# One plan table of a fused linear-attention and feed-forward kernel: own, state and past products put in one place

## The chip, the cores and the metric

The kernel runs on one core of a Trainium2 chip. The metric is the device time of one execution in microseconds (us), as the median over runs. Half a per cent of it (2.7 us) is about what a measurement of this kernel can tell from no change.

## The reference

A recurrence over 768 steps for 4 batches and 8 heads of width 48, and a feed-forward layer with a cosine gate on its output:

```python
for t in range(S):
    cur = u[None] * kt outer vt
    y[:, :, t] = rt . (state + cur)
    state = wt[:, :, :, None] * state + kt outer vt
x = y as (3072 tokens, 384)
h = x @ w_in            # 384 -> 2048
out = (h * cos(h)) @ w_out   # 2048 -> 384
```

Both weights and everything else are float32.

## The kernel before, in words

The 768 steps are cut into 24 chunks of 128 steps (6 per batch, `order`). Two chunks of the same place in two batches make a block (`BLK = 2`), so there are 12 blocks, 0 to 11.

For a chunk, the attention part has these steps, each named by a letter in the plan: `load` (the transposed r, k and w come by DMA into a tile `tt`, five of these), `lr` and `lv` (r and k again for the diagonal, tile `rk`; v, tile `v`, four of these), `decay` (two scans along the chunk on VectorE and the scaling of r and k by them), `diag` (the terms of u: products of `rk` summed to `cd`, L229 to L232, and spread by GpSimd on the diagonal of the score tile `asb`, L236, four of these), `a` (scores k·r on TensorE, L259, then copied under a mask into `asb`, L261), `t` (transposes of k, L268) and `d` (the carried state times the chunk's decay, `dd`, L249, copied to the tiles `past`). For a block it has `o` (the own products: scores times v, L314 and L319, into the banks `py`), `p` (the past products: carried state times r, L329 and L333, added into the same `py`, and then `xT` made from `py`: the high part by ScalarE, the rest by VectorE at L144), and `s` (the state products k·v, L286, into `pst`, then the new state `sn`, L293).

The feed-forward part of a block is 8 units of 256 hidden columns. `mm1` of a unit is 18 matmuls (L382: each product is split in high and low parts, three passes) from `xT` into one of three banks `ph`. A gate follows: L357 on ScalarE, L358 on VectorE, L359 on ScalarE, L360 on VectorE; then `gs`, the high part by a cast on ScalarE and the low part by two subtractions on GpSimd (L144). There are two `gs` tiles, so the cast of unit n waits for `mm2` of unit n-2. `mm2` is 12 matmuls (L401) into `acc`; the first 8 read the high part, the last 4 the low part. `mm2` runs `LAG = 3` units behind `mm1`.

TensorE's order is written out by hand: `START` for the first part, and from then on the eight rows of `PLAN`, one per unit, over and over. A step in a row is emitted where it stands, unless `NEEDS` or the buffer rules in `att` pull it forward: `lv+6` pulls `o` and `s` of the block whose v tile it will overwrite, and a `load` pulls `o`, `s` and `p`. The other engines' orders come from the scheduler, which follows the order of emission and the readiness of data. Rows of `PLAN` set the places for the own products of blocks 3 to 11 (nine blocks); blocks 0 to 2 have theirs in `START`. Blocks 10 and 11 have no state products, since nothing comes after them.

```python
        elif n == "lv":
            att((j - BUFS["v"]) // BLK, "o")
            att((j - BUFS["v"]) // BLK, "s")
```

Of the kernel before, what the change touches and what calls it, by code (L numbers as in the profile page):

```python
# [52 lines left out]
PLAN = ["t+2 t+3 load+6 mm1 mm2",  # L53
        "a+2 mm2 mm1 decay+4",
        "mm2 a+3 mm1 diag+4",
        "mm1 o+1 mm2 diag+5 p+1 lv+6 lr+7 x+2",
        "mm1 s+1 mm2 load+7 lv+7 x+3",
        "mm1 mm2 d+4",
        "mm1 mm2 decay+5",
        "mm1 d+5 mm2 lr+6"]  # L60
# [7 lines left out]
             o="a lv", s="t d lv", p="o d")  # L68
# [637 lines left out]
```

## Time and profile before

| | |
|---|---|
| median of 3 runs | 546.23 us (544.84 to 546.92) |
| the profiled execution | 547.09 us |
| its span in the trace | 545.4 us |
| TensorE (PE) busy | 516.6 us, 95% |
| VectorE (DVE) busy | 368.1 us, 68% |
| ScalarE (ACT) busy | 270.7 us, 50% |
| GpSimd (POOL) busy | 205.0 us, 38% |
| mean granted clock of TensorE | 0.995 |

The span starts with the first instruction in the trace and ends with the last; the profiled execution's own time has 1.7 us more. Times in the rows below are microseconds from the start of the span. PE is the matmuls, PEld the weight loads that run ahead of them. Matmuls overlap in the pipeline, so of a group of matmuls the distance from its start to the start of the next group tells what it costs, rather than its own length.

### The profile page before, as it was taken

The numbers are of one execution on the slowest core, as the hardware profiler recorded it, in microseconds if no ns is written. First come the engines' busy times: TensorE is split into PE (matmuls) and PEld (weight loads), VectorE is DVE, ScalarE is ACT, GpSimd is POOL, SyncE is SP. The second block draws the span as 40 slices with busy tenths as digits, with TensorE's granted clock in tenths as the row PEclk, the third lists the DMA queues.
The fourth block names the chain that finished last, engine by engine and source line by source line (L and its number), as shares of the span: only waits on it lengthen the run. The fifth ranks groups of instructions, "written<-read, shape, count | busy, mean of one in ns | idle before, by whom it ended". The sixth has DMA issues, their size and how long they took to land. (4 is left out here: it accounts for less than half of the span.)

```text
span 545.4 us, 11929 instructions
## 1 busy us (share of the span) xinstructions
PE 516.6 (95%) x4980; PEld 492.9 (90%) x4980; DVE 368.1 (68%) x568; ACT 270.7 (50%) x456; POOL 205.0 (38%) x274
## 2 busy tenths in 40 slices
PE   3668999999899999999999999999999999999996
PEld 3666989989899999999999999999999999999996
DVE  7988999978787477478478478468468664433331
ACT  1778999645343444344444444344344345344542
POOL 4141336653344335335334334334334334323332
PEclk9999999999899999999999999999999999999999
DMA  8984771204370060061061051052032330000000
GB/s 269 277 303 167 240 220 41 77 7 132 117 180 16 30 183 12 30 171 25 30 170 26 30 150 46 30 148 48 29 106 99 131 131 1 31 1 1 30 2 31
DMA packets 16440, 51.38 MB, mean 94 GB/s; under 512 B 1984, under 2 KB 8384, under 8 KB 16384
## 3 DMA queue, kind: packets, MB, share of 16 engines
q1 hardware_dynamic: 16240, 50.49, 30.9%
q8 instruction: 40, 0.66, 0.5%
q14 instruction: 16, 0.13, 0.1%
q10 hardware_dynamic: 144, 0.10, 0.1%
HBM read 45.87 MB, written 4.72 MB: 93 GB/s over the span
## 5 line engine op out<-in xcount | busy, mean ns | idle before, releaser
L144 POOL TENSOR_TENSOR gs<-rr,gs 128x256 fp32r<-128x256 f32 x192 | 159.0, 850 | 228.3 <-ACT gs L141 220.1
L382 PE MATMUL ph<-xT,w 128*128 128x256 f32 x1728 | 225.2, 285 | 6.3 <-ACT w L141 4.8
L382 PEld LDWEIGHTS ph<-xT,w 128*128 128x128 f32 x1728 | 216.5, 192 | 9.8 <-ACT w L141 5.3
L401 PE MATMUL acc<-w,gs 128*128 128x384 f32 x1152 | 218.7, 339 | 1.0 <-DVE rr L360 1.0
L401 PEld LDWEIGHTS acc<-w,gs 128*128 128x128 f32 x1152 | 196.1, 188 | 4.6 <-issue 3.0
L359 ACT ACTIVATE rr<-rr,quarter 128x512 f32<-128x512 f32 x96 | 69.4, 723 | 110.2 <-DVE rr L358 110.0
L358 DVE SCALAR_TENSOR_TENSOR rr<-rr,ph 128x512 f32<-128x512 int32 x96 | 65.5, 682 | 76.2 <-ACT rr L357 63.3
L360 DVE TENSOR_TENSOR rr<-rr,ph 128x512 f32<-128x512 f32 x96 | 65.4, 682 | 46.8 <-ACT rr L359 46.8
L357 ACT ACTIVATE rr<-ph 128x512 int32<-128x512 f32 x96 | 57.1, 595 | 57.6 <-PE ph L382 57.4
L141 ACT CAST gs<-rr 128x512 fp32r<-128x512 f32 x96 | 59.0, 615 | 50.8 <-PE acc L401 40.3
L236 POOL TENSOR_SCALAR_AFFINE_SELECT asb<-cd 128x512 f32<-128x512 f32 x48 | 33.7, 733 | 50.6 <-ACT cd L141 25.6
L261 DVE COPY_PREDICATED asb<-mask,pa 128x512 f32<-128x512 uint8 x48 | 32.9, 735 | 5.8 <-PE pa L259 5.8
L259 PE MATMUL pa<-tt 48*128 48x128 f32 x384 | 32.6, 311 | 1.6 <-ACT ob L414 1.4
L259 PEld LDWEIGHTS pa<-tt 48*128 48x128 f32 x384 | 27.1, 210 | 6.8 <-issue 4.4
L208 DVE TENSOR_TENSOR_SCAN ee<-tt,one_e 112x516 f32<-112x516 f32 x24 | 31.4, 1308 | 1.8 <-DMA tt<-tr 1.8
L213 DVE TENSOR_TENSOR_SCAN tt<-tt,inj 112x516 f32<-112x516 f32 x24 | 31.3, 1303 | 0.1
L141 POOL COPY wholes<-ee 112x4 f32<-112x4 f32 x24 | 10.5, 438 | 54.1 <-DVE ee L208 54.1
L141 ACT COPY past<-dd 48x192 f32<-48x192 f32 x40 | 14.0, 351 | 21.9 <-DVE dd L249 21.3
L224 PEld LDWEIGHTS pc<-u_by_head,rkt 112*128 112x128 f32 x64 | 11.1, 259 | 14.8 <-DVE rkt L205 8.6
L224 PE MATMUL pc<-u_by_head,rkt 112*128 112x2 f32 x64 | 11.3, 299 | 13.6 <-DVE rkt L205 13.1
L217 DVE TENSOR_TENSOR tt<-tt 112x512 f32<-112x512 f32 x24 | 20.0, 833 | 0.1
L229 DVE TENSOR_TENSOR rk<-rk 128x384 f32<-128x384 f32 x16 | 10.9, 680 | 12.4 <-DMA rk<-tn 12.4
(65 smaller groups left out, 346.4 us busy)
## 6 DMA issues: line engine op xcount, KB each, us to landing
tt<-tr SPq DMA_DIRECT2D x22, 674.2 KB, 7.3
raw<-wts SPq DMA_DIRECT2D x16, 768.0 KB, 5.9
rk<-tn SPq DMA_DIRECT2D x16, 384.0 KB, 3.3
v<-tv SPq DMA_DIRECT2D x24, 224.0 KB, 7.0
ww<-w SPq DMA_DIRECT2D x6, 768.0 KB, 4.3
out<-ob SPq DMA_DIRECT2D x23, 192.0 KB, 2.0
tt<-tr SPq DMA_DIRECT2D x4, 224.0 KB, 4.3
tt<-tr SPq DMA_DIRECT2D x2, 226.2 KB, 3.5
```

Source lines behind the costliest of these rows:

```text
L141: (nc.scalar.copy if E[name] is nc.scalar else E[name].tensor_copy)(out=out, in_=in_)
L144: E[name].tensor_tensor(out=out, in0=full, in1=high.bitcast(F32), op=ALU.subtract)
L208: nc.vector.tensor_tensor_scan(out=ee.rearrange("p a t -> p (a t)")[:, ::-1], data0=wp[:, 1:W129 + 1][:, ::-1], data1=one_e.rearrange("p a ...
L236: nc.gpsimd.affine_select(out=asb, in_=col.unsqueeze(2).to_broadcast([C, NP, C]), pattern=[[0, 4], [1, C]], compare_op=ALU.is_equal, fill= ...
L259: nc.tensor.matmul(out=pa[h][:, p], lhsT=a["k3"][rows(h), p], rhs=a["r3"][rows(h), p], start=True, stop=True)
L261: nc.vector.copy_predicated(a["asb", h], mask, pa[h])
L357: nc.scalar.activation(nn, ph, AF.Copy, scale=INV2PI / W_SCALE, bias=0.25)
L358: nc.vector.scalar_tensor_tensor(out=rr, in0=nn, scalar=-2.0 * math.pi * W_SCALE, in1=ph, op0=ALU.mult, op1=ALU.add)
L359: nc.scalar.activation(rr, rr, AF.Sin, scale=1.0 / W_SCALE, bias=quarter)
L360: nc.vector.tensor_tensor(out=rr, in0=rr, in1=ph, op=ALU.mult)
L382: nc.tensor.matmul(out=ph[:, fi], lhsT=wgt[u * FU + fi][:, 0, a, kt * 128:(kt + 1) * 128], rhs=xT[:, b, kt], start=n == 0, stop=n == 3 * K ...
L401: nc.tensor.matmul(out=accs[i][j][:, :DM], lhsT=gs[:, a, fi, j * C:(j + 1) * C], rhs=wgt[u * FU + fi][:, 1, b], start=u == 0 and fi == 0 a ...
```

## The change

Two rows of the plan table are written differently; nothing else is.

```diff
 PLAN = ["t+2 t+3 load+6 mm1 mm2",
         "a+2 mm2 mm1 decay+4",
         "mm2 a+3 mm1 diag+4",
-        "mm1 o+1 mm2 diag+5 p+1 lv+6 lr+7 x+2",
-        "mm1 s+1 mm2 load+7 lv+7 x+3",
+        "mm1 mm2 diag+5 lv+6 lr+7",
+        "mm1 o+1 p+1 s+1 mm2 x+2 load+7 lv+7 x+3",
         "mm1 mm2 d+4",
```

In TensorE's order, in a block in the middle, between `mm1` of unit 3 (the two weight tiles w6 and w7) and `mm1` of unit 4 (w8), there stood before (`py` are the own and past products' banks, `pst` the state's):

```order
L382 MATMUL ph_2130<-xT_1738,w7_616 128x256 x9
L314 MATMUL py_2162<-asb_1614,v_2158 32x128 x2
...
L319 MATMUL py_2163<-asb_1704,v_2160 32x128 x4
L401 MATMUL acc_2196<-w0_181,gs_1989 128x384
...
L329 MATMUL py_2162<-tt_1529,past0_91 32x128 x4
L333 MATMUL py_2162<-tt_1529,past0_91 32x128 x4
...
L286 MATMUL pst_2247<-v_2158,kn_1954 64x48
...
L382 MATMUL ph_2274<-xT_1738,w8_670 128x256 x9
```

and in the same place there stands now:

```order
L382 MATMUL ph_2130<-xT_1761,w7_616 128x256 x9
L401 MATMUL acc_2158<-w0_181,gs_1989 128x384
...
L314 MATMUL py_2184<-asb_1614,v_2180 32x128 x2
...
L319 MATMUL py_2185<-asb_1670,v_2182 32x128 x4
L286 MATMUL pst_2218<-v_2180,kn_1954 64x48
...
L329 MATMUL py_2184<-tt_1529,past0_91 32x128 x4
L333 MATMUL py_2184<-tt_1529,past0_91 32x128 x4
...
L382 MATMUL ph_2274<-xT_1761,w8_670 128x256 x9
```

The own products moved behind the 12 matmuls of `mm2` of unit 0. The state and past products kept their place ahead of `mm1` of unit 4, but the state products, which `lv+6` pulls, now come before the past products, which `lr+7` pulls through its `load`. So `mm1` and `mm2` touch here, and own, state and past products follow one another.

On GpSimd, around the spreading of the diagonal (L236) in a later block, there stood before (`gs_3122` is the low part of unit 2, `gs_3158` that of unit 3):

```order
L144 TENSOR_TENSOR gs_3057<-rr_3052,gs_3057 128x256 x2
L236 AFFINE_SELECT asb_3130<-cd_3128 128x512
...
L236 AFFINE_SELECT asb_3216<-cd_3212 128x512
L144 TENSOR_TENSOR gs_3122<-rr_3117,gs_3122 128x256 x2
L141 COPY wholes_86<-ee_3561 112x4
L141 COPY wholes_86<-ee_3900 112x4
L144 TENSOR_TENSOR gs_3158<-rr_3153,gs_3158 128x256 x2
```

and now:

```order
L144 TENSOR_TENSOR gs_3057<-rr_3052,gs_3057 128x256 x2
L144 TENSOR_TENSOR gs_3122<-rr_3117,gs_3122 128x256 x2
L236 AFFINE_SELECT asb_3130<-cd_3128 128x512
...
L236 AFFINE_SELECT asb_3182<-cd_3178 128x512
L141 COPY wholes_86<-ee_3561 112x4
L141 COPY wholes_86<-ee_3900 112x4
L144 TENSOR_TENSOR gs_3158<-rr_3153,gs_3158 128x256 x2
```

The low part of unit 2 moved ahead of the four spreadings, which therefore come later.

On VectorE, behind those spreadings, in the block of the first pair of fences, the order was (`rr_2293` is the gate of unit 4, `rr_2335` that of unit 5; the second scan L208 reads the tile `tt_2270`):

```order
L232 TENSOR_REDUCE cd_2628<-rk_2451 128x8
...
L229 TENSOR_TENSOR rk_2772<-rk_2772 128x384
...
L229 TENSOR_TENSOR rk_2951<-rk_2951 128x384
...
L358 SCALAR_TENSOR_TENSOR rr_2293<-rr_2293,ph_2274 128x512
L213 SCALAR_TENSOR_TENSOR tt_1963<-tt_1963,inj_80 112x516
L208 SCALAR_TENSOR_TENSOR ee_2900<-tt_2270,one_e_77 112x516
L360 TENSOR_TENSOR rr_2293<-rr_2293,ph_2274 128x512
...
L358 SCALAR_TENSOR_TENSOR rr_2335<-rr_2335,ph_2316 128x512
L213 SCALAR_TENSOR_TENSOR tt_2270<-tt_2270,inj_80 112x516
```

and is now:

```order
L232 TENSOR_REDUCE cd_2628<-rk_2451 128x8
...
L213 SCALAR_TENSOR_TENSOR tt_1963<-tt_1963,inj_80 112x516
L229 TENSOR_TENSOR rk_2772<-rk_2772 128x384
L358 SCALAR_TENSOR_TENSOR rr_2293<-rr_2293,ph_2274 128x512
L217 TENSOR_TENSOR tt_1963<-tt_1963 112x512
L208 SCALAR_TENSOR_TENSOR ee_2900<-tt_2270,one_e_77 112x516
L360 TENSOR_TENSOR rr_2293<-rr_2293,ph_2274 128x512
...
L213 SCALAR_TENSOR_TENSOR tt_2270<-tt_2270,inj_80 112x516
L230 TENSOR_TENSOR rk_2772<-rk_2772,u_sb_84 128x384
L358 SCALAR_TENSOR_TENSOR rr_2335<-rr_2335,ph_2316 128x512
```

So L358 of unit 5 moved behind the second L213, and one of the two products L229 moved behind L358 of unit 5. `sn` and `dd`, which stood behind `xT`, now stand ahead of it. SP's queue changed with them: per block it held `out` twice, `rk` twice, `tt`, `v` twice, `tt`; it now holds `rk`, `v`, `tt`, `v`, `tt`, `rk`, `out` twice.

## Rows read from the trace of the kernel before

**Rows 1.** Windows: length, busy of PE, PEld, DVE, ACT, POOL, clock, DMA, GB/s.
```profile
230.00:275.00 45.00, 45.00 (x493) 43.06 (x495) 29.25 (x47) 19.57 (x35) 15.81 (x23) 1.00 0.25 69
```
**Rows 2.** Timeline of PE, 224 to 254: start, length, group, count.
```profile
224.66 2.25 PE L401 MATMUL acc<-w,gs 128*128 128x384 f32 x12
226.84 1.16 PE L259 MATMUL pa<-tt 48*128 48x128 f32 x16
227.94 4.47 PE L382 MATMUL ph<-xT,w 128*128 128x256 f32 x36
232.34 0.64 PE L314 MATMUL py<-asb,v 128*32 128x128 f32 x16
...
234.22 2.37 PE L401 MATMUL acc<-w,gs 128*128 128x384 f32 x12
236.52 0.64 PE L329 MATMUL py<-tt,past 112*32 112x128 f32 x16
...
237.69 1.13 PE L286 MATMUL pst<-v,kn 128*64 128x48 f32 x32
238.75 2.37 PE L382 MATMUL ph<-xT,w 128*128 128x256 f32 x18
240.96 2.25 PE L401 MATMUL acc<-w,gs 128*128 128x384 f32 x12
243.05 2.26 PE L382 MATMUL ph<-xT,w 128*128 128x256 f32 x18
245.15 2.25 PE L401 MATMUL acc<-w,gs 128*128 128x384 f32 x12
...
253.52 1.73 PE L401 MATMUL acc<-w,gs 128*128 128x384 f32 x9
```
**Rows 3.** Timeline of PEld, same block; in brackets idle before, and why.
```profile
232.69 0.46 PEld L319 LDWEIGHTS py<-asb,v 128*32 128x32 f32 x16
...
234.22 2.05 PEld L401 LDWEIGHTS acc<-w,gs 128*128 128x128 f32 x12 [0.20 <-issue]
236.52 0.38 PEld L329 LDWEIGHTS py<-tt,past 112*32 112x32 f32 x16 [0.25 <-issue]
```
**Rows 4.** Timeline of ACT, same block.
```profile
236.70 0.62 ACT L141 CAST gs<-rr 128x512 fp32r<-128x512 f32 x1 [2.13 <-PE acc L401]
...
250.84 0.60 ACT L141 CAST gs<-rr 128x512 fp32r<-128x512 f32 x1
```
**Rows 5.** Timeline of POOL, same block.
```profile
233.31 2.40 POOL L236 TENSOR_SCALAR_AFFINE_SELECT asb<-cd 128x512 f32<-128x512 f32 x4 [3.34 <-PE py L319]
237.40 1.42 POOL L144 TENSOR_TENSOR gs<-rr,gs 128x256 fp32r<-128x256 f32 x2 [1.69 <-ACT gs L141]
```
**Rows 6.** Timeline of DVE, same block.
```profile
234.57 0.55 DVE L232 TENSOR_REDUCE cd<-rk 128x8 f32<-128x384 f32 x1 [0.75 <-POOL asb L236]
...
238.25 0.98 DVE L229 TENSOR_TENSOR rk<-rk 128x384 f32<-128x384 f32 x1 [1.95 <-DMA rk<-tn]
...
243.42 0.66 DVE L218 TENSOR_TENSOR tt<-tt,ee 112x512 f32<-112x512 f32 x1
...
248.45 1.13 DVE L218 TENSOR_TENSOR tt<-tt,ee 112x512 f32<-112x512 f32 x1
249.50 0.67 DVE L358 SCALAR_TENSOR_TENSOR rr<-rr,ph 128x512 f32<-128x512 int32 x1
250.10 1.22 DVE L213 TENSOR_TENSOR_SCAN tt<-tt,inj 112x516 f32<-112x516 f32 x1
```
**Rows 7.** DMA issues at 237.6 and at 239.2: size, us to landing.
```profile
tt<-tr SPq DMA_DIRECT2D x1, 674.2 KB, 7.0
...
tt<-tr SPq DMA_DIRECT2D x1, 674.2 KB, 9.2
```
**Rows 8.** Timeline of PE, 142 to 150: a wait ahead of scores, then two mm1.
```profile
142.49 1.19 PE L259 MATMUL pa<-tt 48*128 48x128 f32 x14 [1.42 <-ACT ob L414]
143.61 5.98 PE L382 MATMUL ph<-xT,w 128*128 128x256 f32 x36
```

## The prediction

> **What bounds the kernel now.** First the windows: in a stretch of 45 us in the middle TensorE is busy for all 45, VectorE for 29, ScalarE for 20 and GpSimd for 16, at the full granted clock [rows 1]. So TensorE is the bound there, and nothing is to be won by making another engine faster. Then its timeline, where busy can hide small losses: I read the distance from the start of a group to the start of the next [rows 2]. An `mm1` behind an `mm2` takes 2.10 us (243.05 to 245.15), one behind float32 products of other shapes 2.21 (238.75 to 240.96). An `mm2` takes 2.18 between an `mm1` and other products (224.66 to 226.84), 2.30 between two kinds of other products (234.22 to 236.52). So each change of kind costs about 0.1 us on either side of it. The weight loads show the same: inside the own products they follow without a pause, and at a change they idle 0.20 to 0.25 us [rows 3]. The last view is of the other engines behind the own products, since they hold the gates that TensorE needs later [rows 4 to 6].
>
> **The change on TensorE.** No matmul is added or removed; one `mm2` and the own products change places, and state and past products do. Per block:
> - The two `mm1` of units 2 and 3 take 4.40 us before (227.94 to 232.34), because own products follow. Now `mm2` follows: 2.21 + 2.10 = 4.31 [rows 2]. Gain 0.09.
> - `mm2` of unit 0 stood between own and past products, 2.30; now it stands between `mm1` and own products, 2.18. Gain 0.12.
> - Own (1.88), past (1.17) and state products (1.06) stay as long, by the starts of [rows 2]. Each of the three ended on a change of kind or shape before, which its distance contains, and each does now.
>
> That is 0.21 us in each of the nine blocks that the table places: 9 x 0.21 = 1.9 us. In blocks 10 and 11, which have no state products, own and past products of one width now touch; what that saves is nothing at least and one pause of 0.20 each at most [rows 3], 0 to 0.4 together. I take 0.2. The changes from own to state and from state to past products are in no row. The nearest are the pauses of 0.20 and 0.25 [rows 3]; a change may cost one pause more or one less than the one that it replaces, so 7 x 0.2 = 1.4 us to either side in the seven blocks with state products. I take none, since every change of shape in the rows lies within 0.05 us of the others. Sum: 2.1 us, with bounds of 0.5 and 3.7.
>
> A rule speaks here against this order of the products. The Trainium skill (TensorEngine Tiling (Array Packing), Key Properties) says that changing the tiling mode drains the engine, while changing the tile within a mode does not; state products, with 64 columns, thus break up own and past products, which have 32. By it the boundaries fall from six to five per block, and from five to three in the last two blocks, 7 + 4 = 11 in all; at a pause of 0.20 that would be 2.2 us, and the order own, past, state would have saved more.
>
> **The change on the other engines.** `mm2` of unit 0 ends 2.09 us earlier, at 234.43 instead of 236.52, so the cast of unit 2, which waited for it (2.13 us of idle, released by `acc`), comes at 234.6 instead of 236.70 [rows 4]. Own products start at 234.43 instead of 232.34. The spreading on GpSimd waited for them before. Now it also stands behind the low part of unit 2, which starts at 237.40 - 2.09 = 235.3 and takes 1.42 [rows 5]. So it starts at 236.7 instead of 233.3, two of its four parts end at 236.7 + 2.40 / 2 = 237.9, and VectorE's first `cd`, which waits for them, starts at 238.0 instead of 234.57 [rows 6]: 3.4 us later.
>
> From there VectorE runs without a gap to L358 of unit 5. Before, that distance was 249.50 - 234.57 = 14.93 us. Now the wait for `rk` (1.95) falls away, since other work stands ahead of it; one product L229 (0.98) has moved behind; the second scan L213 (1.22) has moved ahead [rows 6]. That makes 13.2, or 12.7 where L218 takes 0.66 as it does without GpSimd beside it, rather than 1.13. So L358 of unit 5 starts at 250.7 to 251.2, where it started at 249.50. ScalarE's cast of unit 4 stands behind it and ended 1.94 us after its start (250.84 + 0.60) [rows 4]; it ends at 252.6 to 253.1. `mm2` of unit 4 needs that cast at 253.52 - 0.21 = 253.3 [rows 2]. **A margin of 0.2 to 0.7 us is left of the 2.1 that there were.** Of everything that moves later this is the tightest: I take the cost as nothing, covered by `mm2` and `mm1` of the units between, and if the cover goes, every further microsecond on VectorE is one of TensorE.
>
> On SP's queue the first `rk` waits for that `cd` (238.6), and `v` and the `tt` that the second scan reads stand behind it, each some 0.5 us apart (four issues stood between 237.6 and 239.2): `tt` is issued at 239.6 rather than 237.64. A `tt` took 7.0 us to land in that place, and 9.2 as the last of the queue [rows 7]. It lands at 246.6, or at 248.8. The second scan is due some 4.5 us ahead of L358 of unit 5 (two scans, L360, L218 and L230 lie between; an estimate from the 1.22 and 0.66 of [rows 6] and about 0.6 for each of the others), at 246.2 to 246.7. I take 7.0, because only one `rk` and one `v` are ahead of it, and so a wait of 0 to 0.4 us on VectorE, within the margin. Loads of `v`, the second `rk` and the results are needed a block later or microseconds after this, and cost nothing. The unit's other casts and the release of the `ph` banks keep over 2 us each.
>
> **The sum.** The profiled execution took 547.09 us, 1.7 more than its span, and the change takes 2.1 off: 545.0. The median of the runs shown is 546.23, 0.9 below that execution. The prediction is for a median: 546.23 - 2.1 = **544.1 us**, 0.4% less, with 542.5 to 545.7 by the bounds.
>
> **Rivals.**
> - *A late gate takes the place of the saved changes (slower).* Place: `mm2` of unit 4 waiting for the cast, released by ScalarE behind VectorE's second scan behind `tt`. It decides from a landing of about 7.6 us on. At 9.2 us the scan is 2.1 to 2.6 late, less 0.2 to 0.7 of margin: some 1.9 us of stall in seven blocks with such a load, +13.3 - 2.1, so 557 us. At 8.2 us it is some 0.9 a block, so 6.3 - 2.1 more than now, 550.4 us; at 7.9 us it is 0.6, 548.3. For it: the margin is a third or less of what it was. Against it: fewer bytes are ahead of this `tt` than ahead of the one with 9.2. A wait of 1.42 us at 142.49 was followed by two `mm1` of 5.98 us instead of 4.47 [rows 8], which a wait here might repeat, at 1.5 us each. The Trainium skill (SBUF — State Buffer, Who interferes with whom) adds that a VectorE instruction with two SBUF inputs and a GpSimd instruction that reads SBUF shut each other out for a whole instruction. The rows agree as far as L218 goes, 0.66 alone and 1.13 beside a low part. By that rule the loss could be a whole half of a low part, 0.71 instead of 0.47, and the margin would be gone. Chance 0.13.
> - *The gain is eaten (no change).* The same wait, at 7.6 to 8 us of landing: 0.3 us a block, 7 x 0.3 = 2.1, so 546.2 us. Chance 0.17.
> - *The changes of shape cost more than I count (faster).* At the upper bound, 3.7 us: 542.5 us. For it: pauses of 0.25 occur. Against it: the order keeps state products between the others. Chance 0.12.
> - *The change does nothing.* Excluded by the order: `mm2` and own products do change places in nine blocks.
>
> **How the numbers follow.** The forecast has the remaining 0.58. Half a per cent is 2.7 us (below 543.5 or above 548.96), about what a measurement of this kernel can tell from no change. The forecast at 2.1 lies near that edge and runs differ by 1 us, so I give a fifth of it (0.12) and nearly all of the faster rival to faster: 0.23. Slower is the late gate beyond some 8 us, 0.12. Same is 0.65. The range reaches from the upper bound, 542.5, over the eaten gain to a gate that is late by 0.2 us in seven blocks beyond it, 547.5; it leaves out the late gate and little else.
>
> **What would show it.** A block on TensorE should shrink by 0.2; the two `mm1` should take 4.3, `mm2` of unit 0 2.18; no idle of PE should stand ahead of L401 behind ScalarE's cast. The `cd` should come some 3.4 us later in the block. I am wrong if PE waits at `mm2` of unit 4, or VectorE at L208 for `tt` by more than half a microsecond, or if the change from own to state products takes over 0.3 us.

## The result, and the profile after

The change makes the kernel slower: 549.74 us (median of 7 runs, 548.52 to 552.51) against 545.34 us for the kernel before in the same series (544.84 to 548.02). The ratio estimated from the runs is 1.0069, with a 95% interval of 1.0052 to 1.0087; the two medians alone give 1.0081. The profiled execution took 550.04 us, its span is 548.3.

The same stretch as in [rows 1], with the same columns, no longer has TensorE busy throughout; 0.7 us of 45 are idle:

```profile
230.00:275.00 45.00, 44.32 (x446) 41.99 (x446) 28.19 (x46) 19.10 (x35) 14.93 (x22) 1.00 0.27 69
```

The view of waits of the kernel after (who waited for whom, us in total, times, longest) has two entries that matter. In the kernel before, the wait of L208 for `tt` was 1.8 us, once, in the start, and no matmul waited for the cast `gs`:

```profile
DVE ee L208 <- DMA tt<-tr: 6.1, 6, 1.8
...
PEld acc L401 <- ACT gs L141: 3.6, 5, 0.9
...
PE acc L401 <- ACT gs L141: 2.6, 5, 0.7
```

The timeline of PE after, of the block that answers to [rows 2]:

```profile
227.62 4.47 PE L382 MATMUL ph<-xT,w 128*128 128x256 f32 x36
231.93 2.25 PE L401 MATMUL acc<-w,gs 128*128 128x384 f32 x12
234.12 0.64 PE L314 MATMUL py<-asb,v 128*32 128x128 f32 x16
...
236.00 1.13 PE L286 MATMUL pst<-v,kn 128*64 128x48 f32 x32
237.06 0.65 PE L329 MATMUL py<-tt,past 112*32 112x128 f32 x16
...
238.23 2.39 PE L382 MATMUL ph<-xT,w 128*128 128x256 f32 x18
240.46 2.24 PE L401 MATMUL acc<-w,gs 128*128 128x384 f32 x12
...
246.72 2.26 PE L382 MATMUL ph<-xT,w 128*128 128x256 f32 x18
248.82 2.52 PE L401 MATMUL acc<-w,gs 128*128 128x384 f32 x12
251.17 2.26 PE L382 MATMUL ph<-xT,w 128*128 128x256 f32 x18
254.12 1.15 PE L401 MATMUL acc<-w,gs 128*128 128x384 f32 x5 [0.68 <-ACT gs L141]
```

By the starts, the pair of `mm1` takes 4.31 and `mm2` of unit 0 2.19: the saving is there. It is lost at the end: `mm2` of unit 3 takes 2.35 (248.82 to 251.17) instead of 2.09 (in the other four blocks of this kind it takes 2.09), and `mm2` of unit 4 waits for the cast. What the cast waits for stands in the timelines of DVE, of POOL and of ACT, same block (to compare with [rows 4 to 6]), and in the DMA issue at 239.12:

```profile
237.63 0.55 DVE L232 TENSOR_REDUCE cd<-rk 128x8 f32<-128x384 f32 x1 [2.64 <-POOL asb L236]
...
245.24 0.68 DVE L217 TENSOR_TENSOR tt<-tt 112x512 f32<-112x512 f32 x1
247.34 1.23 DVE L208 TENSOR_TENSOR_SCAN ee<-tt,one_e 112x516 f32<-112x516 f32 x1 [1.42 <-DMA tt<-tr]
248.49 0.66 DVE L360 TENSOR_TENSOR rr<-rr,ph 128x512 f32<-128x512 f32 x1
...
249.16 0.91 DVE L218 TENSOR_TENSOR tt<-tt,ee 112x512 f32<-112x512 f32 x1
249.99 1.76 DVE L213 TENSOR_TENSOR_SCAN tt<-tt,inj 112x516 f32<-112x516 f32 x1
251.68 0.53 DVE L230 TENSOR_TENSOR rk<-rk,u_sb 128x384 f32<-128x384 f32 x1
252.13 0.68 DVE L358 SCALAR_TENSOR_TENSOR rr<-rr,ph 128x512 f32<-128x512 int32 x1
```
```profile
235.00 1.42 POOL L144 TENSOR_TENSOR gs<-rr,gs 128x256 fp32r<-128x256 f32 x2 [5.42 <-DVE rr L360]
236.37 2.40 POOL L236 TENSOR_SCALAR_AFFINE_SELECT asb<-cd 128x512 f32<-128x512 f32 x4
...
248.63 0.19 POOL L141 COPY wholes<-ee 112x4 f32<-112x4 f32 x1 [6.83 <-DVE ee L208]
248.78 1.89 POOL L144 TENSOR_TENSOR gs<-rr,gs 128x256 fp32r<-128x256 f32 x2
```
```profile
253.47 0.60 ACT L141 CAST gs<-rr 128x512 fp32r<-128x512 f32 x1
```
```profile
tt<-tr SPq DMA_DIRECT2D x1, 674.2 KB, 8.2
```

Read upwards from the cast: it follows L358 of unit 5 (252.13), that stands behind L230 and the second L213, that behind the second L208, and this one waited 1.42 us for a `tt` that landed 8.2 us after its issue at 239.12. L213 took 1.76 us instead of the 1.22 of [rows 6], because the low part of unit 3 ran beside it: GpSimd has that low part behind the small copy of `ee` into `wholes`, which waits for the same second L208.

Block by block (start of the pair of `mm1` to the next; a block is counted by the own products that stand at its pair, so the first is block 3): before, blocks 4 to 8 take 41.38 to 41.42 us; after, 42.14, 42.51, 41.89, 42.19 and 41.42 from 185.48 on, 3.15 more in all. Over the whole trace the start is 0.56 earlier, the nine blocks are 2.94 longer, the end is 0.58 longer: 2.96 us, the difference of the spans. The medians differ by 4.4; the profiled execution of the kernel before (547.09) was slower than its median, so the traces account for 3.0 of these. The mean granted clock is 0.978 against 0.995, but it is lower only in the first 55 us, and TensorE starts the pair of block 3 at 143.05, earlier than before (143.61), so that is no part of the difference of the spans.

### The profile page after: what moved, and what is told of

It reads as the page before. It is cut to its first block, busy times and chain, and to the rows that moved or that the text cites. A ratio compares the mean times of both kernels' runs of the same rounds, so it can differ in the third digit from the quotient of the medians.

```text
span 548.3 us, 11906 instructions
## 1 busy us (share of the span) xinstructions
PE 514.3 (94%) x4980; PEld 490.2 (89%) x4980; DVE 367.5 (67%) x568; ACT 268.6 (49%) x456; POOL 200.7 (37%) x274
## 5 line engine op out<-in xcount | busy, mean ns | idle before, releaser
L144 POOL TENSOR_TENSOR gs<-rr,gs 128x256 fp32r<-128x256 f32 x192 | 156.6, 837 | 246.9 <-ACT gs L141 207.5
L358 DVE SCALAR_TENSOR_TENSOR rr<-rr,ph 128x512 f32<-128x512 int32 x96 | 65.4, 682 | 71.2 <-ACT rr L357 56.3
L236 POOL TENSOR_SCALAR_AFFINE_SELECT asb<-cd 128x512 f32<-128x512 f32 x48 | 34.2, 744 | 24.8 <-ACT cd L141 24.8
L213 DVE TENSOR_TENSOR_SCAN tt<-tt,inj 112x516 f32<-112x516 f32 x24 | 34.8, 1450 | 0.1
L208 DVE TENSOR_TENSOR_SCAN ee<-tt,one_e 112x516 f32<-112x516 f32 x24 | 30.5, 1272 | 6.1 <-DMA tt<-tr 6.1
L141 POOL COPY wholes<-ee 112x4 f32<-112x4 f32 x24 | 8.7, 361 | 67.9 <-DVE ee L208 67.9
L232 DVE TENSOR_REDUCE cd<-rk 128x8 f32<-128x384 f32 x16 | 8.8, 552 | 24.1 <-POOL asb L236 24.1
L224 PE MATMUL pc<-u_by_head,rkt 112*128 112x2 f32 x64 | 10.5, 286 | 13.6 <-DVE rkt L205 13.1
L218 DVE TENSOR_TENSOR tt<-tt,ee 112x512 f32<-112x512 f32 x24 | 18.7, 777 | 0.0
```

Source lines behind the costliest of these rows:

```text
L141: (nc.scalar.copy if E[name] is nc.scalar else E[name].tensor_copy)(out=out, in_=in_)
L144: E[name].tensor_tensor(out=out, in0=full, in1=high.bitcast(F32), op=ALU.subtract)
L213: nc.vector.tensor_tensor_scan(out=wp[:, 0:W129], data0=wp[:, 0:W129], data1=inj.rearrange("p a t -> p (a t)"), initial=0.0, op0=ALU.mult, ...
L236: nc.gpsimd.affine_select(out=asb, in_=col.unsqueeze(2).to_broadcast([C, NP, C]), pattern=[[0, 4], [1, C]], compare_op=ALU.is_equal, fill= ...
L358: nc.vector.scalar_tensor_tensor(out=rr, in0=nn, scalar=-2.0 * math.pi * W_SCALE, in1=ph, op0=ALU.mult, op1=ALU.add)
```

## The experiments

Three theories of the wait came out of this trace: 1, the later chain (own products, and so `cd`, come later); 2, the order (state ahead of past products brings L213 and L230 ahead of L358 of unit 5); 3, the tile (the second scan waits for `tt`). For each there are kernels that part it from the others. The diffs are in the plan table or the tables beside it, and in the last two kernels also in the loop that emits the plan. Two kernels, with the kernel before and the change, make a square: own products early or late, and past or state products first.

**State before past products alone**

```diff
 (against the kernel before)
-        "mm1 o+1 mm2 diag+5 p+1 lv+6 lr+7 x+2",
+        "mm1 o+1 mm2 s+1 diag+5 p+1 lv+6 lr+7 x+2",
```

> Own products stay at their place of before, behind the second mm1 of the pair and ahead of mm2 of unit 0; only state and past products change places, state ahead of past. On TensorE no distance should shrink (the pair of mm1 stays at 4.4, mm2 of unit 0 at 2.3), so nothing is gained there. Theory 1, the late chain (the stall comes because own products stand one mm2 later, and so the spreading on GpSimd and the first cd on VectorE come 3.4 us later): no wait of mm2 of unit 4 for the cast gs, 545.3 us like before, within 1. Theory 2, the order (state ahead of past sends the second L213 and L230 ahead of L358 of unit 5 on VectorE): the wait of 0.4 to 0.7 us a block is still there, +3 to +5 us. Theory 3, the tile (the second scan waits for tt, which lands 7.8 us after its issue): no wait beyond that of before, since tt is issued as early as before, 545.3.

Measured: 547.64 us, ratio 1.0023 (1.0009 to 1.0038). No matmul waits for the cast, and blocks take 41.38 to 41.43; the 1.1 us by which its span is longer lie ahead of 187 us, and where they come from was not settled. So theory 2 falls as a cause by itself. But theory 3 was wrong in its detail: `tt` is freed by the past products, which now end one group later, so it was issued 10.8 instead of 9.7 us after the pair, and the scan did wait. The timeline of DVE:

```profile
247.30 1.23 DVE L208 TENSOR_TENSOR_SCAN ee<-tt,one_e 112x516 f32<-112x516 f32 x1 [1.30 <-DMA tt<-tr]
...
249.95 1.76 DVE L213 TENSOR_TENSOR_SCAN tt<-tt,inj 112x516 f32<-112x516 f32 x1
...
252.08 0.67 DVE L358 SCALAR_TENSOR_TENSOR rr<-rr,ph 128x512 f32<-128x512 int32 x1
```

**Own products late alone**

```diff
 (against the kernel before)
-        "mm1 o+1 mm2 diag+5 p+1 lv+6 lr+7 x+2",
+        "mm1 mm2 o+1 diag+5 p+1 lv+6 lr+7 x+2",
```

> Own products one mm2 later as in the change, but past products right behind them and state products last: own and past products, of one width, touch. On TensorE the pair of mm1 should take 4.3, mm2 of unit 0 2.2, own to past 1.77 instead of 1.88: 0.32 us a block less than before, 2.9 us over nine blocks, if nothing waits. VectorE has L358 of unit 5 ahead of the second L213 again, as before; GpSimd has the low part of unit 2 ahead of the spreading, as in the change. Theory 1, the late chain: cd comes 3.4 us late here too, but 1.76 of scan and some 0.6 of L230 have left the chain ahead of L358 of unit 5; the stall shrinks to 0 to 0.3 us a block and the time is 542.4 to 545. Theory 2, the order: no stall at all, 542.4. Theory 3, the tile: a wait of VectorE at L208 for tt as in the change (1 us a block), and a stall of 0.3 or more, 545 to 547.

Measured: 544.39 us, ratio 0.9965 (0.9951 to 0.9980): faster than both. Blocks without a wait take 41.04 to 41.07, 0.35 less than before. The cast of unit 4 is never late, although `cd` comes as late as in the change: L358 of unit 5 stands ahead of the second L213 here. So theory 1 falls as a cause by itself too. Two blocks have a stall, of 0.44 us in the one from 143.21 and of 0.92 in the one from 309.43 (42.23 us), where `tt` landed after 8.2 us; what was late then was not the cast but the low part of unit 4:

```profile
337.49 0.62 PE L401 MATMUL acc<-w,gs 128*128 128x384 f32 x2 [0.92 <-POOL gs L144]
```

The square, as the end of the cast of unit 4 after the start of the pair, and when `mm2` of unit 4 needs it (one block of each, starting at 227.94, 229.12, 227.32 and 227.62):

| | past first | state first |
|---|---|---|
| own early | 23.50, needed 25.58 | 24.90, needed 25.58 |
| own late | 23.56, needed 25.24 | 26.45, needed 25.37 |

The table mixes the orders with the landings of these four blocks: 1.30 of the 1.40 us that state first costs alone, and 1.42 of the 2.95 of both together, are the wait of L208 for `tt`. Without that wait the cast ends at 23.51 (before), 23.35 (own late, block from 186.26), 23.62 (state first, block from 187.69, less its wait of 0.17) and 24.92 (both: the control below, which has the orders of the change, block from 311.17). So each move alone costs 0.1 us at most, and together they take 1.4 of the 2.08 that were spare before any landing is late. A later `cd` fills the waits that VectorE has behind it: 1.95 us for `rk` before [rows 6], 1.41 us for `pst` with state first. But state first also brings L213 and L230 ahead of L358 of unit 5 and sends `tt` later, so both moves and the landing draw on the same 2.08 us.

**A sixth tile `tt`, and its control**

```diff
 (against the change; the control has only kn=2 and rr=5)
-BUFS = dict(tt=5, v=4, h=2, rd=2, rr=7, gs=2, asb=4, sn=4, xT=2, kn=4, ...
+BUFS = dict(tt=6, v=4, h=2, rd=2, rr=5, gs=2, asb=4, sn=4, xT=2, kn=2, ...
-        "mm1 mm2 diag+5 lv+6 lr+7",
+        "mm1 mm2 diag+5 lv+6 p+1 lr+7",
```

> The change with a sixth tile tt, so that a load of tt overwrites a tile used longer ago, paid with two tiles kn instead of four and five rr instead of seven; TensorE's order is that of the change but for the last two blocks, where own and past products come one mm1 earlier. Theory 3, the tile: with the load free of the late chain the wait of VectorE at L208 for tt (6.1 us in six places) goes, the wait of mm2 of unit 4 for the cast gs falls from 0.4 to 0.7 to 0.1 or less, and the time is 544 to 546. Theory 1 and 2: half of the stall or more stays, as the chain behind cd is late by 3.4 us and the second scan still stands ahead of L358 of unit 5: 547 to 549. If it is above 550, the smaller kn and rr cost something of their own, to be told by a run with these two alone.

> The change with two kn and five rr instead of four and seven, and five tt as before: the control of the run with six tt. Every engine's order is that of the change. If the sixth tt was what removed the stalls, the wait of VectorE at L208 for tt (about 6 us, six places) and the wait of mm2 of unit 4 for the cast (2.6 us, five places) are back, and the time is that of the change, 549 to 551. If the smaller kn and rr had removed them, the time is 546. In the run with six tt a pair of mm1 took 4.34 us instead of 4.31 and a block 0.2 to 0.3 us more than its groups should; if that comes from where the tiles lie, a pair takes 4.34 here too, and the time is 1 to 2 us above the change.

Measured: with six `tt` 546.10 us, ratio 0.9992 (0.9978 to 1.0005); the control 548.63, ratio 1.0049 (1.0026 to 1.0072). With six, L208 waits only in the start and no matmul waits for the cast; L358 of unit 5 starts 13.1 us after `cd` (237.40 to 250.53) instead of 14.5. So the wait for `tt` is a necessary part of the stall. One caution: the scheduler also put the second scan ahead of L358 of unit 4 there, which leaves the sum ahead of L358 of unit 5 the same.

The control is the more instructive one. Its twelve runs lie between 546.42 and 552.66, and the profiled one is the lowest; with every engine's order as in the change, three of its blocks have no stall at all. VectorE in the block from 227.54, where `tt` landed after 6.8 us:

```profile
245.81 1.24 DVE L208 TENSOR_TENSOR_SCAN ee<-tt,one_e 112x516 f32<-112x516 f32 x1
...
247.62 0.92 DVE L218 TENSOR_TENSOR tt<-tt,ee 112x512 f32<-112x512 f32 x1
248.46 1.76 DVE L213 TENSOR_TENSOR_SCAN tt<-tt,inj 112x516 f32<-112x516 f32 x1
...
250.60 0.68 DVE L358 SCALAR_TENSOR_TENSOR rr<-rr,ph 128x512 f32<-128x512 int32 x1
```

Ten blocks of the two traces, in order of when `tt` landed, show dose and response:

| kernel, block | `tt`: issue after the pair + time to landing | wait at L208 | wait of `mm2` of unit 4 | block |
|---|---|---|---|---|
| control, 311.17 | 11.46 + 6.4 | 0 | 0 | 41.18 |
| control, 352.35 | 11.46 + 6.6 | 0 | 0 | 41.20 |
| control, 227.54 | 11.46 + 6.8 | 0 | 0 | 41.20 |
| change, 354.21 | 11.49 + 7.1 | 0.31 | 0 | 41.42 |
| control, 185.81 | 11.46 + 7.5 | 0.66 | 0.17 | 41.73 |
| change, 270.13 | 11.77 + 7.3 | 0.48 | 0.30 | 41.89 |
| change, 185.48 | 11.50 + 7.8 | 1.04 | 0.59 | 42.14 |
| change, 312.02 | 11.49 + 7.9 | 1.09 | 0.63 | 42.19 |
| control, 268.74 | 11.69 + 7.9 | 1.36 | 0.68 | 42.43 |
| change, 227.62 | 11.50 + 8.2 | 1.42 | 0.68 | 42.51 |

In the seven of these blocks with a wait at L208, and in the five blocks from 187 us on of the kernel with state first alone, the cast of unit 4 ends 6.74 to 6.77 us after the landing. So once the scan waits, the landing alone sets the cast, and in the change the later `cd` counts through the issue of `tt`: `cd` ends at 238.18, the first `rk` is issued at 238.21, `tt`, two places behind it on SP's queue, at 239.12.

**The copy `wholes` on VectorE**

```diff
 (against the change)
-LATER = dict(whole="p", pc0="a", ...
+LATER = dict(whole="v", pc0="a", ...
```

> The change with the small copy of ee into wholes on VectorE instead of GpSimd. GpSimd's low part of unit 3 stood behind that copy, which waits for the second scan L208, and so ran beside the second L213, which then took 1.76 us instead of 1.22. Now the low part can start with its cast, some 1.8 us earlier. If the shared access is part of the stall: L213 back at 1.22 and L218 at 0.66 in most blocks, the wait of mm2 of unit 3 for the low part (2.35 instead of 2.09) gone, and the stall of mm2 of unit 4 smaller by 0.3 to 0.7 us a block, so gone or nearly: 545 to 547. VectorE pays 0.2 us twice a block for the copies, and L230 moves behind L358 of unit 5 (0.44 less ahead of it). If the tile tt alone makes the stall, the wait at L208 (1.0 us a block) stays and so does a stall of 0.3 us a block or more: 548 to 549.

Measured: 545.57 us, ratio 0.9986 (0.9970 to 1.0002), so some 4 us below the change. VectorE and GpSimd, in the block from 187.02 (`tt` landed after 7.5 us):

```profile
206.05 1.23 DVE L208 TENSOR_TENSOR_SCAN ee<-tt,one_e 112x516 f32<-112x516 f32 x1 [0.67 <-DMA tt<-tr]
...
208.46 0.68 DVE L218 TENSOR_TENSOR tt<-tt,ee 112x512 f32<-112x512 f32 x1
209.07 1.22 DVE L213 TENSOR_TENSOR_SCAN tt<-tt,inj 112x516 f32<-112x516 f32 x1
210.21 0.65 DVE L358 SCALAR_TENSOR_TENSOR rr<-rr,ph 128x512 f32<-128x512 int32 x1
```
```profile
206.14 2.38 POOL L144 TENSOR_TENSOR gs<-rr,gs 128x256 fp32r<-128x256 f32 x2 [7.98 <-ACT gs L141]
```

The low part starts with the scan L208, is done before L213, and L213 is back at 1.22. The cast of unit 4 ends 6.1 us after the landing instead of 6.75. Those 0.65 are a sum: 0.77 less in L218 and L213, 0.45 less because L230 now stands behind L358 of unit 5, and 0.59 more for the copy on VectorE (207.87 to 208.46). Waits for `tt` of 0.36 to 0.72 us are still there in three of the five blocks from 187 to 393 us, and only one of these is longer for it (41.49; the others take 41.19 to 41.22). So a chain that is 0.65 us shorter behind the landing nearly ends the stall. That the shared access alone would do it was not shown, since L230 moved too.

**All three products early, and two versions of its end**

```diff
 (against the kernel before)
-        "mm1 o+1 mm2 diag+5 p+1 lv+6 lr+7 x+2",
-        "mm1 s+1 mm2 load+7 lv+7 x+3",
+        "mm1 o+1 p+1 s+1 mm2 diag+5 lv+6 lr+7 x+2",
+        "mm1 mm2 load+7 lv+7 x+3",
```

> Own products at their place of before; past and state products follow them directly, and mm2 of unit 0 comes behind all three (2.2 us later than before). By the distances measured so far own to past takes 1.77 instead of 1.88, mm2 of unit 0 2.2 instead of 2.3, and mm1 of unit 4, now behind an mm2, 2.10 instead of 2.23: 0.32 us a block less than before, 2.9 us in all. Theory 1: the spreading comes no later than before, so no wait for the cast of unit 4: 542.4 us, faster than both kernels. Theory 2: state products are behind past products and ahead of mm2, past ahead of state as before: no stall either, 542.4. If it is above 545, a later mm2 of unit 0 (and with it the cast and low part of unit 2) costs what the own products gain.

Measured: 548.11 us, ratio 1.0036 (1.0019 to 1.0053). Blocks 4 to 8 do what was expected, 41.04 to 41.07 without a stall. Block 10 takes 44.07 instead of 39.55. Its own products have their place of before; what moved is VectorE. The second pair of copies to `asb` stands behind one `top` (L350) more than in the kernel before, and that one waits for its DMA, so the copies start 7.19 us after the pair instead of 3.50. PE, then DVE:

```profile
440.08 0.43 PE L314 MATMUL py<-asb,v 128*32 128x128 f32 x8 [3.12 <-DVE asb L261]
```
```profile
437.64 1.75 DVE L350 TENSOR_REDUCE top<-ww 128x1 f32<-128x1536 f32 x1 [2.31 <-DMA ww<-w]
439.31 1.33 DVE L261 COPY_PREDICATED asb<-mask,pa 128x512 f32<-128x512 uint8 x2
```

The two versions keep the early place for blocks 3 to 9 and move own and past products of the last two blocks back:

```diff
 (against all three early; the first version keeps x+2 in the upper row)
-        "mm1 o+1 p+1 s+1 mm2 diag+5 lv+6 lr+7 x+2",
-        "mm1 mm2 load+7 lv+7 x+3",
+        "mm1 o+1 p+1 s+1 mm2 diag+5 lv+6 lr+7",
+        "mm1 o+1 p+1 mm2 x+2 load+7 lv+7 x+3",
...
                 n, _, d = e.partition("+")
+                if n in "op" and i + 1 >= NBLK - 2 and row == PLAN[3]:
+                    continue
```

> As the run with own, past and state products early and together, but in the last two blocks own and past products stand behind mm1 of unit 4, where the change has them. That run gained 0.35 us a block up to block 9 and lost 3.1 us in block 10, where own products waited for asb behind a top (L350) that waited for its DMA. If that wait was the whole loss, the own products of block 10 come some 4.3 us later, behind L261, and do not wait; the time is nine blocks of 0.33 to 0.35 us below before, 543.4 us, ratio 0.994 to 0.995. If the loss moves to another gate of the last two blocks, ratio 0.998 or more.

> As the run with own, past and state products early but the last two blocks apart; there x+2 at the end of the row before had pulled own and past products to directly behind mm2 of unit 0, 2.2 us later than early, not behind mm1 of unit 4, and own products of block 10 still waited 0.87 us for asb (block of 40.3 us instead of 39.2). Here x+2 stands in the next row, so own and past products of the last two blocks stand behind mm1 of unit 4, where the change has them, another 2.1 us later. If asb behind top (L350) was the last loss, block 10 takes 39.2 to 39.5 us and the time is 1 us lower than that run's, 543.2 us, ratio 0.994. If tops hold up another gate there, as in the change (block 10 took 39.9 with a wait of 0.19 for ob), there is no gain over that run, ratio 0.996.

Measured: the first 544.22 us, ratio 0.9961 (0.9946 to 0.9976), block 10 at 40.29 with a wait of 0.87 for `asb`; the second 543.56 us, ratio 0.9949 (0.9933 to 0.9966), block 10 at 39.21, no such wait. It beats both kernels of this case. PE in a middle block of it:

```profile
225.54 4.47 PE L382 MATMUL ph<-xT,w 128*128 128x256 f32 x36
229.94 0.64 PE L314 MATMUL py<-asb,v 128*32 128x128 f32 x16
...
231.71 0.62 PE L329 MATMUL py<-tt,past 112*32 112x128 f32 x16
...
232.86 1.13 PE L286 MATMUL pst<-v,kn 128*64 128x48 f32 x32
233.92 2.36 PE L401 MATMUL acc<-w,gs 128*128 128x384 f32 x12
236.12 2.26 PE L382 MATMUL ph<-xT,w 128*128 128x256 f32 x18
238.22 2.25 PE L401 MATMUL acc<-w,gs 128*128 128x384 f32 x12
```

Own to past products take 1.77 instead of 1.88 (229.94 to 231.71), `mm2` of unit 0 2.20, the `mm1` behind it 2.10; in this block nothing is late: own products are where they were and past products earlier.

## Why the prediction was wrong

Forecast were 544.1 us, 2.1 less than before, with a range up to 547.5; measured are 549.74, 4.4 more than before in the same series.

- **The change on TensorE: right.** Forecast were 0.21 us a block. Blocks of the control without a stall take 41.20 against 41.40. The pairs, `mm2` of unit 0, and own (1.88), state (1.06) and past products (1.17) have the forecast distances, so the change from own to state products has no price of its own. The Trainium skill (TensorEngine Tiling (Array Packing), Key Properties) was read as saying that own, past, state would save more: by the blocks of own products late alone, 41.04 to 41.07, it is some 0.14 us more, so the trace agrees.
- **The later chain: right.** `cd` came 10.01 us after the pair (forecast 238.0 - 227.94 = 10.06). In the control's block without a wait L358 of unit 5 starts at 23.06 (forecast 22.8 to 23.3) and the cast ends at 25.0 (24.7 to 25.2), due at 25.39 (forecast 25.4). The margin of 0.2 to 0.7 us was 0.4. In part that is luck: the second L213 took 1.76, not 1.22, and the rest of the chain was as much shorter.
- **The step that failed: "I take 7.0, because only one `rk` and one `v` are ahead of it, and so a wait of 0 to 0.4 us on VectorE, within the margin."** The issue was forecast well (239.6, that is 11.66 after the pair; 11.5 measured). The landing took 7.1 to 8.2 us in the five blocks of the change, mean 7.7, and 6.4 to 7.9 in the control, mean 7.0. So one row was taken for a quantity that scatters by 1.5 us in the control, against a margin of 0.4, and a late landing costs while an early one returns nothing. The cost "as nothing" is then the mean of what exceeds the margin, not what exceeds it at the mean. More rows of the kernel before would not have shown the tail: in its five blocks from 186.54 on this `tt` landed after 6.2, 7.0, 6.5, 6.9 and 7.0 us, so the 7.0 was already the highest there (the quickest stands below this list). Nor does the reason given hold, that few loads are ahead: with own products late alone only one `rk` is ahead of this `tt`, and it landed after 5.1 to 8.2. Against the block of 41.20 the five blocks lost 0.94, 1.31, 0.69, 0.99 and 0.22, together 4.15 us.
- **The rival that came true was named, at its place, and mispriced.** It was to decide from a landing of 7.6 us; the table has it between 7.1 and 7.5 at the issue of 11.5. It was to cost 0.6 a block at 7.9, in seven blocks; it cost 0.99 there, and five blocks had a wait at L208. At 8.2, a wait of 0.68 made a block 1.31 longer: 0.26 in `mm2` of unit 3, whose low part is held by the same scan, 0.85 in the `mm1` with the wait behind it (251.17 to 254.12 instead of 2.10), and about 0.2 in the `mm2` behind that. The slow pair of [rows 8] was not repeated: the granted clock stood at the lower level (0.50, 1.2 GHz) from 143.5 to 146.9 us there, and at 1.00 from 187 to 500 us in the change, with all its waits of `mm2` for the cast.
- **Blocks 9 and 10 were not looked at.** They lost more than they saved and are 0.29 and 0.33 us longer than before (40.89 and 39.88), with waits of 0.40 for the cast and 0.19 for `ob`. That `top` and its DMA are behind these is argued from their place on VectorE; it was tried only for own products, in the last two kernels.

The issue at 196.25 in the kernel before, the quickest of its five:

```profile
tt<-tr SPq DMA_DIRECT2D x1, 674.2 KB, 6.2
```

Why this `tt` landed 0.7 us later in the change than in the control, with the same orders, and why later in either than in the kernel before, was not settled. There is one trace of each, and that of the control is its fastest execution.

## What to carry to other kernels

When a move eats most of a margin, list everything that still draws on it, and take for each transfer the spread over all blocks instead of one row: a one-sided cost starts as soon as the tail passes the margin. Even that spread belongs to its place in the queue: here it was 6.2 to 7.0 before and 7.1 to 8.2 after, so a margin of 0.4 was too small to rely on. Moving work later can be free only as long as another engine's idle wait hides it; two moves that are each free may use the same wait. Where groups can be joined by moving one earlier or another later, the earlier place keeps the margins, but look at the last rounds, where other work shares the engines.

## What the runs showed of the hardware that was not expected

- The same load in the same place of the order landed after 6.4 to 7.9 us within one execution, and with six `tt`, issued 12 to 13 us after the pair, after 5.0 to 8.3.
- A scan L213 that started while a low part was running took 1.76 us in every such block from 185 to 394 us of the change, the control and the kernel with state first alone, 1.22 where none ran (1.46 with six `tt`); L218 took 0.92 instead of 0.66. Beside the scan L208, which started 0.09 us before it (206.05, 206.14), it was the low part that gave way: 2.38 instead of 1.42, L208 1.23. The Trainium skill (SBUF — State Buffer, Who interferes with whom) says that the order of issue decides who is blocked; these rows agree.
- With six `tt` a pair of `mm1` took 4.34 instead of 4.31 and a block 41.44 to 41.48, although nothing waited; the control had 4.31. Why is open.
